# Joined shift copies, a shared Gelu session and a new planning string in a two-layer transformer kernel

## The chip, the cores and the metric

The kernel runs on one core of one Trainium2 chip. The metric is the device time of one execution in microseconds; less is better. The kernel before has a median of 1543.89 us over three runs.

## The reference

Two layers, each made of softmax attention and a two-matrix network, with a residual around each and a layer normalisation before each. Both layers use the same weights. The input x is 2048 tokens of 512 channels in bf16; there are 32 heads of 16 channels, and the hidden width F is 1376.

```python
def _A_ref(x, wqkv, wo):
    ...
    scores = jnp.einsum("bhqd,bhkd->bhqk", q, k) * scale
    p = _softmax(scores, axis=-1)
    o = jnp.einsum("bhqk,bhkd->bhqd", p, v)
    return o.transpose(0, 2, 1, 3).reshape(B, S, D) @ wo

def _B_ref(x, w1, b1, w2, b2):
    y = _layernorm(x, axis=-1)
    h = _gelu(jnp.einsum("bsd,df->bsf", y, w1) + b1)
    return jnp.einsum("bsf,fd->bsd", h, w2) + b2

x = A_x
x = x + _A_ref(_layernorm(x, axis=-1), A_wqkv, A_wo)
x = x + _B_ref(_layernorm(x, axis=-1), B_w1, B_b1, B_w2, B_b2)
# and the same two steps once more
```

## The kernel before

The program is not written out by hand. A planner in Python (the class `Sched`) runs while the kernel is built: jobs, written as generators, hand it tasks for TensorE (pe), ScalarE (act), VectorE (dve), GpSimd (pool) and SyncE (sp, the DMA queue), each with a priority (lower goes first), a planned duration and the buffers it reads and writes. `best` picks for every engine the task of best priority among those that are ready by the engine's planned free time plus a small look-ahead (0.05 us on VectorE). The result is one fixed instruction stream per engine with semaphore waits; at run time nothing is chosen any more. So a planned duration moves instructions in the order, and has no other effect. A second pass (`refill`) puts multiplications by zeros into planned holes of TensorE's stream.

**The score tiles.** The work is cut into segments: for each layer (called 1 and 3 in the code), each unit of query tokens (up to 512; layer 3's last unit is cut into 256, 128 and 128) and each group of four heads. A segment has a tile of 128 keys x 512 queries for every key block and head. There are 4096 such tiles of exponentials in all, and two ways to make one.

- ScalarE: an Exp over three or two score banks at once (line 1493), written to the buffer `PT`. One multiplication per tile then accumulates it with V (line 1701).
- VectorE, for five of every sixteen key blocks only: `d_load` (line 1594) turns the scores of one tile into bit patterns of bf16 numbers, by adding a constant and writing integers. A pair of tiles (`DBATCH` is 2) fills one slot u of the buffer `dp`, 1024 integers a partition. `job_d` then makes the shifted copies: a first shift (line 1625) writes slot u+1 as slot u plus a constant, 1024 elements; a second shift (line 1630) writes the two slots v, v+1 as slots u, u+1 plus another constant, 2048 elements. A tile so made is accumulated four times, with V and three scaled copies of V (`vs`). A few pairs are closed half filled, and their shifts have half the elements.

`flow_scores` decides at each step, tile by tile, which engine gets the next ones (`take_d`, `d_solo`), by the planned backlog of VectorE and the free slots. Its thresholds come from the class `Hint`: every fourth group of ScalarE reads one character of the string `ORDER`, which picks one of ten sets of thresholds (`MODES`). The string has 315 characters.

**Priorities on VectorE.** A score eviction has 0.0, the transpose that empties the accumulator bank 0.3, a shift 2.5 as a rule, and 0.5 or 0.15 when its segment runs out.

**The rest of a layer.** `job_segend` normalises a segment, `job_post` multiplies by wo, adds the residual, normalises again, and starts `job_ffn` for the unit. `job_ffn` multiplies by w1 chunk by chunk (`mm_w1`, line 1836), adds the bias on VectorE (line 1860) into the buffer `h16`, and then runs Gelu over the whole buffer on ScalarE (lines 1875 and 1876). Exp and Gelu need different tables, so each such session stands between two table loads. The multiplication by w2 follows (line 1883), then the residual (line 1885) and, for layer 3, the store of the output. There is one `h16`, so a unit's session must be over before the next unit's chunks come in. `job_tail` does the same for the last 128 tokens in its own way.

**Buffers.** `dp` has 14 slots of 1024 integers; the second half of the buffer `OT`, a tensor of its own, is lent as two more (14 and 15) in the middle of each layer. Free slots, in pairs, are handed out in the order in which they were freed. `qk` and `xnT` are buffers for making q, k and v, and are not used after layer 3's are made.

Of the kernel before, what the change touches and what calls it, by code (L numbers as in the profile page):

```python
# [63 lines left out]
class Prog:  # L64


    def __init__(self):
        self.streams = {e: [] for e in ENGINES}
        self.last_writer = {}
        self.readers = {}  # L70
        self.ops = []
        self.dma_rr = 0
        self.free = {e: 0.75 for e in ENGINES}
        self.bus = 0.0
        self.spare = tuple
        self.tiling = "full"
        self.tiles = {}
        self.drain = 0.0
        self.hit = (0.0, 0.0, 0.0)
        self.work = []  # L80
# [25 lines left out]
    def op(self, eng, fn, reads=(), writes=(), same_ok=(), dur=0.3, lat=None):  # L106
# [32 lines left out]
        else:  # L139
            if eng == "pool":  # L140
                self.hit = (op.t0, op.t0 + dur, lat or 0.0)
                lat = None
            elif lat == "fast":
                if self.hit[0] < op.t0 + dur and op.t0 < self.hit[1]:
                    dur += self.hit[2]
                lat = None
# [109 lines left out]
class Task:  # L256

    __slots__ = ("eng", "ops", "prio", "cb", "seq")

    def __init__(self, eng, prio, ops):  # L260
        self.eng = eng
        self.prio = prio
        self.ops = ops
        self.cb = None
        self.seq = 0

# [12 lines left out]
class Sched:  # L279
# [80 lines left out]
    def release(self, name, slot):  # L360
# [5 lines left out]
        if p.waiters:  # L366
            _, _, cb = heapq.heappop(p.waiters)
            cb(slot)
        else:
            p.free.append(slot)  # L370

# [74 lines left out]
    def run(self):  # L446
        while True:
# [19 lines left out]
            for (fn, reads, writes, same_ok, dur, lat) in t.ops:  # L467
                self.P.op(t.eng, fn, reads, writes, same_ok, dur, lat)
            if t.cb is not None:
                t.cb()  # L470
# [6 lines left out]
AHEAD = 0.3  # L477
HOLD_REACH = 1.0
# [40 lines left out]
DOT = True  # L519


class Hint:
    BASE = dict(D_IDLE=1.2, PV_LEAST=0.75, HOLD_LATE=0.4, PV_NEAR=0.7, LIN2=9, D_STEAL=0)
    MODES = (dict(), dict(D_IDLE=0.8), dict(D_IDLE=1.7), dict(PV_LEAST=0.6), dict(PV_LEAST=0.9), dict(HOLD_LATE=0.2), dict(HOLD_LATE=0.6), dict(PV_NEAR=0.4), dict(LIN2=0.9), dict(D_STEAL=1.0))
    STEP = 4
    ORDER = '503313558500015300210144501302104000000301040403092343050392450495084100003032530945249044022459044803755795410000404059000042073300979450905900455532342400007300030045005594475501306437245071003021030010012714080892409008554010031403031302434070022009444030045044310000030072220934002201909240590090394095010099504'
# [13 lines left out]
class Builder:  # L540
# [45 lines left out]
    def alloc(self, es):  # L586
# [31 lines left out]
        self.dp = t("dp", [128, NDP, 1024], U16)  # L618
        self.vs = t("vs", [128, 3, 3, len(DK), 68], BF16)
        self.OT = t("OT", [128, 8, 512], BF16)  # L620
# [85 lines left out]
    def otd(self, hg):  # L706

        return [("dp", NDP + (hg - 4) // 2, w) for w in (0, 1)] if DOT and hg >= 4 else []

    def dpu(self, u):  # L710

        return self.dp[:, u, :] if u < NDP else self.OT[:, 2 * (u - NDP) + 4:2 * (u - NDP) + 6, :].rearrange("p a n -> p (a n)").bitcast(U16)

    def dpp(self, u):

        return self.dp[:, u:u + 2, :] if u < NDP else self.OT[:, 4:8, :].rearrange("p a n -> p (a n)").bitcast(U16).rearrange("p (u n) -> p u n", u=2)
# [143 lines left out]
    def flow_weights(self):  # L860
# [17 lines left out]
        for qc in range(self.NC + 1):  # L878
            L = 1 if qc < self.NC else 3
            if qc:  # L880
                yield ("keys", [("post", 1, qc - 1)])
            for fc in range(self.NFC):
                yield first(fc)
                S_.mark(("w1", L, qc % self.NC, fc))
            if L == 1:
# [14 lines left out]
    def ln_group(self, tiles, slot, prio, eps1, eps0, shift):  # L900
# [14 lines left out]
        if shift:  # L915
            nmr = self.nmr[:, c0:c0 + n]
            yield Task("pool", prio, [I(lambda e: e.tensor_tensor(out=nmr, in0=self.mv[:, c0:c0 + n, 0], in1=rs, op=ALU.mult), [R] + [("mv", c0 + i) for i in range(n)], [("nmr", slot)], 0.2),
                                      I(lambda e: e.tensor_scalar(out=nmr, in0=nmr, scalar1=-1.0, scalar2=None, op0=ALU.mult), [("nmr", slot)], [("nmr", slot)], 0.2)])
# [142 lines left out]
    def bound(self, x, y, a, c, ns, dst, RQ, RN, prio, eng):  # L1061
# [4 lines left out]
        yield Task("dve", prio, [I(lambda e: e.tensor_scalar(out=yi, in0=x.bitcast(I32), scalar1=-0.5, scalar2=RSQRT_MAGIC, op0=ALU.mult, op1=ALU.add), RN, [RY], 0.18)])  # L1066
        yield Task(eng, prio, [I(lambda e: e.tensor_tensor(out=a, in0=x, in1=y, op=ALU.mult), RN + [RY], [RA], 0.25 if pool else 0.2)])
        yield Task(eng, prio, [I(lambda e: e.tensor_tensor(out=c, in0=a, in1=y, op=ALU.mult), [RA, RY], [RC], 0.25 if pool else 0.2)])
        yield Task(eng, prio, [I(lambda e: e.tensor_scalar(out=c, in0=c, scalar1=-0.5, scalar2=1.5, op0=ALU.mult, op1=ALU.add), [RC], [RC], 0.217 if pool else 0.2)])
        yield Task(eng, prio, [I(lambda e: e.tensor_tensor(out=a, in0=a, in1=c, op=ALU.mult), [RA, RC], [RA], 0.25 if pool else 0.2)])  # L1070
        yield Task(eng, prio, [I(lambda e: e.tensor_scalar(out=dst, in0=a.rearrange("p (n o) -> p n o", o=1), scalar1=-MARG, scalar2=0.0, op0=ALU.mult, op1=ALU.add),
                                    [RA], [RQ], 0.333 if pool else 0.2)])
# [108 lines left out]
    def job_scl(self, L, part, prio):  # L1181
# [19 lines left out]
        yield Task("dve", prio, [I(lambda e: e.tensor_scalar(out=self.krhs[:, :], in0=self.mask8[:, :], scalar1=self.kmx[:, 1:2], scalar2=None, op0=ALU.mult), [("kmx", 1), ("mask8",)], [("krhs",)], 0.1)])  # L1201
# [23 lines left out]
    def job_qt(self, sg, s):  # L1225
# [9 lines left out]
                                  [RS, ("scl", k), ("qbias",)], [("qt", q)], 0.16 + 0.24 * W / 512 if eng == "dve" else 0.41 + 0.48 * W / 512, (), "fast" if eng == "dve" else 0.09)])  # L1235
# [8 lines left out]
    def job_vs(self, sg, i, kbs):  # L1244
# [9 lines left out]
        if L == 1:  # L1254
# [5 lines left out]
                                   [("V", hg, kb) for kb in kbs], [("vs", q, i + k2) for k2 in range(n)], 0.209 + 0.17 * n, [("vs", q, i + k2) for k2 in range(n)] if k > 1 else [], 0.09) for k in (1, 2, 3)])  # L1260
# [321 lines left out]

    def close_batch(self):
# [35 lines left out]
    def job_d(self, bt):  # L1619
# [5 lines left out]
        yield Task("dve", prio(), [I(lambda e: e.tensor_scalar(out=self.dpu(u + 1)[:, 0:N], in0=self.dpu(u)[:, 0:N], scalar1=float(SHIFT[1]), scalar2=None, op0=ALU.add),  # L1625
                                     [("dp", u, w) for w in range(n)], [("dp", u + 1, w) for w in range(n)] + self.dres(u + 1), 0.150 + 0.2605e-3 * N, (), "fast")])
        self.d_ready(bt, 1, u + 1, u, range(n))
        v = yield ("get", "dp", sg["i"])
        self.need2 -= 1
        yield Task("dve", prio(), [I(lambda e: e.tensor_scalar(out=self.dpp(v)[:, :, 0:N], in0=self.dpp(u)[:, :, 0:N], scalar1=float(SHIFT[2]), scalar2=None, op0=ALU.add),  # L1630
                                     [("dp", u + i, w) for i in (0, 1) for w in range(n)], [("dp", v + i, w) for i in (0, 1) for w in range(n)] + self.dres(v) + self.dres(v + 1), 0.150 + 0.521e-3 * N, (), "fast")])
        for i in (0, 1):
# [91 lines left out]
    def job_segend(self, sg):  # L1724
# [15 lines left out]
        if nparts == 2 and part == 0:  # L1740
            yield Task("dve", 1.2, [I(lambda e: e.tensor_copy(out=self.rowA[:, hg, :], in_=T[:, :, 17]), [RA], [("rowA", hg)], 0.17)])
# [5 lines left out]
        if nparts == 2:  # L1747
# [4 lines left out]
            yield Task("pool", 1.2, [I(lambda e: e.tensor_tensor(out=M, in0=M, in1=dw.unsqueeze(2).broadcast_to([128, 16, 16]), op=ALU.mult), [RW] + RO, RO, 0.62, (), 0.28),  # L1752
# [30 lines left out]

    def post_prio(self, L, qc):

        return 0.95 if L == 1 and qc >= self.NC - 2 or L == 3 and qc >= LATE3 else 2.2

    def job_post(self, L, qc):
# [28 lines left out]
        if self.prev(L, qc):  # L1817
# [14 lines left out]
    def mm_w1(self, L, qc, fc, b, pr, W, y0=0):  # L1832
        M = 128 if fc < self.NFC - 1 else self.FLAST
        yield ("keys", [("w1", L, qc, fc)])
        for c0 in (0, 2):
            yield Task("pe", pr if c0 == 0 else min(pr, HINT.LIN2), [I(lambda e, c=c: e.matmul(self.ps[0:M, b, 0:W], lhsT=self.w1(fc, c), rhs=self.yT[:, c, y0:y0 + W], start=(c == 0), stop=(c == 3)),  # L1836
# [7 lines left out]
    def job_ffn(self, L, qc):  # L1844
# [6 lines left out]
        hv = self.gv  # L1851
        yield ("keys", [("retq", 2), ("retq", 3), ("rets", 1)])
        for fc in range(NFC):
# [6 lines left out]
            S_.submit(Task("dve", pr - 0.7, [I(lambda e, fc=fc, M=M, b=b: e.tensor_scalar(out=hv[0:M, fc * W:(fc + 1) * W], in0=self.ps[0:M, b, 0:W], scalar1=self.b1c[0:M, fc:fc + 1], scalar2=None, op0=ALU.add),  # L1860
                                               [("ps", b), ("b1c",)], self.hres(fc * W // 512), 0.2 + 0.54 * W / 512, [("h", fc * W // 1024)])]),
                      cb=lambda b=b, fc=fc: (S_.release("mb", b), S_.mark(("h", L, qc, fc))))
        S_.mark(("ffn1", L, qc))
        yield ("keys", [("h", L, qc, fc) for fc in range(NFC)])
        HR = [("h", k) for k in range((NFC * W + 1023) // 1024)]
# [9 lines left out]
        yield Task("act", -1.0, [I(lambda e: e.activation(out=self.gv[:, 0:nf * W], in_=hv[:, 0:nf * W], func=ACTF.Gelu_apprx_tanh), HR, HR, (0.2 if last else 1.5) + 0.427 * nf * W / 512, (), (0.2 if last else 1.513) + 0.427 * nf * W / 512),  # L1875
# [3 lines left out]
        for i, tt in enumerate(tiles):  # L1879
            yield ("ready", "pe", GR + [r for fc in range(NFC) for r in self.w2res(L, fc)])  # L1880
            b = yield ("get", "mb")
            for f0 in range(0, NFC, 2):
                yield Task("pe", pr if f0 == 0 else min(pr, HINT.LIN2), [I(lambda e, fc=fc, i=i, b=b: e.matmul(self.ps[:, b, :], lhsT=self.gt(fc, i, W), rhs=self.w2(L, fc), start=(fc == 0), stop=(fc == nf)),  # L1883
                                        GR + self.w2res(L, fc), [("ps", b)], 0.216, [("ps", b)]) for fc in range(f0, min(f0 + 2, NFC))])
# [197 lines left out]
```

## Time and profile before

| | |
|---|---|
| median of three runs (lowest, highest) | 1543.89 us (1541.95, 1544.90) |
| the profiled execution, own time | 1542.35 us |
| its span, first to last instruction | 1540.5 us |
| ScalarE: exponentials, L1493 | 1258 instructions, 1421.4 us |
| ScalarE: all Gelu over `h` and `g`, L1875 and L1876 | 18 instructions, 40.0 us |
| ScalarE: table loads | 18, of 1283 ns each |
| VectorE: score evictions, L1594 | 983 instructions, 655.7 us |
| VectorE: first shifts, L1625 | 495 instructions, 210.5 us |
| VectorE: second shifts, L1630 | 495 instructions, 342.7 us |

In the profile's groups a line number names the line of the kernel that issued the instruction; engines are PE (TensorE), PEld (its weight loads), DVE (VectorE), ACT (ScalarE), POOL (GpSimd), SP (the DMA queue). Durations are those of single instructions, and neighbours on one engine can overlap, so sums of durations can exceed the time taken. The buffer `h16` appears as `h`, `g10` as `g`. The profiler's spans of GpSimd are rough.

### The profile page before, as it was taken

How to read it: one execution, taken by the hardware profiler on the slowest of the kernel's cores; microseconds unless marked ns; L12 is line 12 of the kernel's file. 1: busy time of each engine (PE TensorE's matmuls, PEld its weight loads, DVE VectorE, ACT ScalarE, POOL GpSimd, SP SyncE). 2: the span in 40 equal slices, each digit the busy share in tenths (PEclk: the TensorE clock that was granted, in tenths of full speed). 3: DMA queues.
4: the chain of work that ended last, by engine and by line, in shares of the span. 5: the costliest groups of instructions: out<-in, count | busy, mean ns of one | idle time of the engine just before them, and what ended most of it. 6: DMA issues, size and time to landing. Idle time of an engine off the chain costs nothing.

```text
span 1540.5 us, 41172 instructions
## 1 busy us (share of the span) xinstructions
PE 1490.5 (97%) x17581; PEld 489.7 (32%) x17581; DVE 1459.9 (95%) x2857; ACT 1505.1 (98%) x1348; POOL 331.0 (21%) x570
## 2 busy tenths in 40 slices
PE   8999999999999999999999999999999999999998
PEld 3222222222222222232222322222222222344565
DVE  8899999999999899999999898999999999999896
ACT  8999999999999999999999999999999999999997
POOL 3686322001220021102322217320001000020200
PEclk9999999999999999999999999999999999999999
DMA  6673012213311132223832332310101100221221
GB/s 164 118 157 87 26 29 35 55 31 76 87 46 48 41 69 74 60 49 82 153 51 62 64 69 71 62 25 22 29 19 36 35 18 24 41 41 33 66 67 30
DMA packets 212488, 90.56 MB, mean 59 GB/s; under 512 B 182251, under 2 KB 207184, under 8 KB 212304
## 3 DMA queue, kind: packets, MB, share of 16 engines
q1 hardware_dynamic: 212304, 87.92, 26.0%
q8 instruction: 138, 2.26, 0.6%
q14 instruction: 46, 0.38, 0.1%
HBM read 36.81 MB, written 19.48 MB: 37 GB/s over the span
## 4 chain that ended last, share of the span: by engine, by line
ACT 47%; DVE 25%; PE 23%; issue 2%; POOL 2%; DMA 1%; SPq 0%; POOLq 0%; DVEq 0%
ACT PT L1493 44%; DVE dp L1594 9%; PE ps L1508 7%; PE ps L1701 6%; DVE dp L1630 4%; PE ps L1883 3%; DVE dp L1625 2%; PE ps L988 2%; ACT h L1875 2%; PE ps L1836 2%; PE ps L1397 1%; DVE accT L1731 1%; DVE n L1053 1%; DVE h L1860 1%; DVE OT L1594 1%
## 5 line engine op out<-in xcount | busy, mean ns | idle before, releaser
L1493 ACT ACTIVATE PT<-ps 128x1536 bf16<-128x1536 f32 (+1 forms) x1258 | 1421.4, 1302 | 19.8 <-PE ps L1508 16.8
L1594 DVE TENSOR_SCALAR dp<-ps 128x512 uint16<-128x512 f32 x899 | 599.2, 682 | 32.6 <-PE ps L1508 29.9
L1508 PE MATMUL ps<-QT,KT 32*128 32x512 bf16 (+2 forms) x5120 | 602.1, 339 | 24.5 <-ACT PT L1493 7.4
L1701 PE MATMUL ps<-PT,V 128*17 128x512 bf16 (+2 forms) x3891 | 478.0, 338 | 0.1
L1701 PE MATMUL ps<-dp,vs 128*17 128x512 bf16 (+2 forms) x3377 | 438.9, 336 | 1.5 <-issue 0.6
L1508 PEld LDWEIGHTS ps<-QT,KT 32*128 32x128 bf16 x5120 | 175.0, 91 | 543.1 <-ACT PT L1493 290.9
L1630 DVE TENSOR_SCALAR dp<-dp 128x2048 uint16<-128x2048 uint16 x404 | 280.5, 699 | 2.9 <-PE ps L1701 0.2
L1234 POOL TENSOR_SCALAR QT<-qraw,scl,qbias 128x512 bf16<-128x512 bf16 (+2 forms) x91 | 73.0, 802 | 813.8 <-PE ps L1508 811.1
L1701 PE MATMUL ps<-dp,V 128*17 128x512 bf16 (+2 forms) x1135 | 210.8, 337 | 1.3 <-DVE accT L1731 0.7
L1625 DVE TENSOR_SCALAR dp<-dp 128x1024 uint16<-128x1024 uint16 (+1 forms) x453 | 192.7, 436 | 2.3
L1701 PEld LDWEIGHTS ps<-dp,vs 128*17 128x17 bf16 x3377 | 115.7, 89 | 110.5 <-issue 81.0
L1701 PEld LDWEIGHTS ps<-PT,V 128*17 128x17 bf16 x3891 | 122.6, 89 | 87.8 <-issue 71.4
L1401 PE MATMUL ps<-zw 128*32 128x448 bf16 (+21 forms) x1389 | 150.1, 323 | 0.3 <-DVE dp L1594 0.2
L1399 PE MATMUL ps<-zw 32*128 32x444 bf16 (+5 forms) x379 | 117.6, 331 | 0.0
L1836 PE MATMUL ps<-yT,wf 128*128 128x512 bf16 (+5 forms) x440 | 101.5, 340 | 2.7 <-DMA yT<-xn 1.4
L1397 PE MATMUL ps<-zw 128*128 128x448 bf16 (+15 forms) x382 | 96.8, 341 | 3.1 <-DVE onec L783 2.1
L988 PE MATMUL ps<-wqkv,xnT 128*128 128x512 bf16 x336 | 93.7, 382 | 3.9 <-DVE qk L1001 1.0
L1701 PE MATMUL ps<-OT,vs 128*17 128x512 bf16 (+2 forms) x310 | 79.0, 360 | 0.0
L1860 DVE TENSOR_SCALAR h<-ps,b1c 128x512 bf16<-128x512 f32 (+4 forms) x99 | 65.6, 666 | 4.5 <-PE ps L1836 3.9
L1259 POOL TENSOR_SCALAR vs<-V 128x340 bf16<-128x340 bf16 (+2 forms) x72 | 62.4, 867 | 29.8 <-PE ps L1701 20.9
L1701 PEld LDWEIGHTS ps<-dp,V 128*17 128x17 bf16 x1135 | 52.7, 88 | 34.0 <-issue 17.5
L1731 DVE STREAM_TRANSPOSE accT<-ps 128x512 f32<-128x512 f32 (+2 forms) x96 | 59.3, 618 | 2.3 <-PE ps L1701 2.3
(197 smaller groups left out, 1169.4 us busy)
## 6 DMA issues: line engine op xcount, KB each, us to landing
vs<-vs_scr SPq DMA_DIRECT2D x64, 255.0 KB, 2.8
wf<-in_B_w_dram SPq DMA_DIRECT2D x90, 128.0 KB, 2.4
q_scr<-qk SPq DMA_DIRECT2D x20, 256.0 KB, 2.0
k_scr<-qk SPq DMA_DIRECT2D x12, 256.0 KB, 2.0
out_dram<-xres SPq DMA_DIRECT2D x16, 128.0 KB, 1.7
vs_scr<-vs SPq DMA_DIRECT2D x8, 255.0 KB, 2.7
xres<-in_A_x_dram SPq DMA_DIRECT2D x7, 256.0 KB, 3.6
v_scr<-vst SPq DMA_DIRECT2D x12, 136.0 KB, 1.9
```

Source lines behind the costliest of these rows:

```text
L988: yield Task("pe", prio if c0 == 0 else min(prio, HINT.LIN2), [I(lambda e, c=c: e.matmul(self.ps[:, b, :], lhsT=xnT[:, c, :], rhs=self.wqk ...
L1397: fn = lambda e: e.matmul(self.ps[:, b, 0:w], lhsT=self.zw[:, 0:128], rhs=self.zw[:, 0:w], start=st, stop=st, skip_group_check=True)
L1399: fn = lambda e: e.matmul(self.ps[:, b, 0:w], lhsT=self.zw[32 * p:32 * p + 32, 0:128], rhs=self.zw[32 * p:32 * p + 32, 0:w], start=st, sto ...
L1401: fn = lambda e: e.matmul(self.ps[32 * p:32 * p + 32, b, 0:w], lhsT=self.zw[:, 0:32], rhs=self.zw[:, 0:w], start=st, stop=st, skip_group_c ...
L1493: S_.submit(Task("act", 1e-5 * gi, [I(lambda e, pt=pt, n=n, b0=b0: e.activation(out=self.PT[:, pt:pt + n, :], in_=self.ps[:, b0:b0 + n, :] ...
L1508: return [I(lambda e, kb=kb, i=i: e.matmul(self.ps[:, b, i * W:(i + 1) * W], lhsT=self.KT[32 * hp:32 * hp + 32, hg, kb * 128:(kb + 1) * 12 ...
L1594: self.S_.submit(Task("dve", 0.0, [I(lambda e: e.tensor_scalar(out=self.dpu(u)[:, w * 512:(w + 1) * 512], in0=self.ps[:, b, :], scalar1=BI ...
L1625: yield Task("dve", prio(), [I(lambda e: e.tensor_scalar(out=self.dpu(u + 1)[:, 0:N], in0=self.dpu(u)[:, 0:N], scalar1=float(SHIFT[1]), sc ...
L1630: yield Task("dve", prio(), [I(lambda e: e.tensor_scalar(out=self.dpp(v)[:, :, 0:N], in0=self.dpp(u)[:, :, 0:N], scalar1=float(SHIFT[2]), ...
L1701: ops.append((nth[j, sh] + 0.1 * i, I(lambda e, hp=hp, v=v, ap=ap[:, i * W:(i + 1) * W], first=first and i == 0, W=W: e.matmul(self.ps[32 ...
L1836: yield Task("pe", pr if c0 == 0 else min(pr, HINT.LIN2), [I(lambda e, c=c: e.matmul(self.ps[0:M, b, 0:W], lhsT=self.w1(fc, c), rhs=self.y ...
L1860: S_.submit(Task("dve", pr - 0.7, [I(lambda e, fc=fc, M=M, b=b: e.tensor_scalar(out=hv[0:M, fc * W:(fc + 1) * W], in0=self.ps[0:M, b, 0:W] ...
```

## The change

1. **Joined shifts.** A shift task of a whole pair carries a mark (`mate`): its kind and its slots. When the planner issues one, it looks for another of the same kind on VectorE that is ready within the look-ahead and whose slots stand in the same order; if there is one, both go out as one instruction over two pieces of memory (`both`, `d_join`), planned 0.15 us shorter than the sum. For this `dp` and `OT` become one tensor `bits` (18 slots, the lent pair is now 16 and 17), and free pairs are handed out lowest first.
2. **Shared session.** `HELD` names layer 3's unit 0 as held for unit 1. Unit 0's biased chunks go into `qk` and `xnT`; its Gelu, w2 multiplication, residual and stores follow with those of unit 1, in one session between two table loads. Two short memsets prepare the row that carries the second bias. Unit 1 no longer waits for the end of unit 0.
3. **Planner.** The model of how GpSimd slows a VectorE instruction looks at GpSimd's last four instructions instead of one. Some twenty planned durations change by 0.02 to 0.3 us, nearly all upwards.
4. **String and priorities.** `Hint` gets two more modes (`POST`), which change the priority of `job_ffn`'s multiplications, and a new `ORDER` of 315 characters, 60 of them as before at their place. After the last score group w1 multiplications get priority 1.3, and the last-but-one unit's residual additions 3.0.

```diff
@@ Sched.release
             p.free.append(slot)
+            if name == "dp":
+                p.free.sort()
@@ Prog.op
             if eng == "pool":
-                self.hit = (op.t0, op.t0 + dur, lat or 0.0)
+                self.hits = self.hits[-3:] + [(op.t0, op.t0 + dur, lat or 0.0)]
...
-                if self.hit[0] < op.t0 + dur and op.t0 < self.hit[1]:
-                    dur += self.hit[2]
+                dur += sum(h for t0, t1, h in self.hits if t0 < op.t0 + dur and op.t0 < t1)
@@ Sched.run
+            both = None
+            if t.mate is not None:
+                lim = max(pick[0], self.P.free["dve"]) + self.LOOK["dve"]
+                both = next((o for o in self.pend["dve"] if o.mate is not None and o.mate[0] == t.mate[0] and (o.mate[1] < t.mate[1]) == (o.mate[2] < t.mate[2]) and self.task_ready(o) <= lim), None)
+            if both is not None:
+                self.pend["dve"].remove(both)
+                (fn, reads, writes, same_ok, dur, lat), more = t.ops[0], both.ops[0]
+                x, y = sorted((t.mate[1:], both.mate[1:]))
+                self.P.op("dve", self.join(t.mate[0], x, y), reads + more[1], writes + more[2], same_ok, dur + more[4] - SHIFT_FIXED, lat)
+                for o in sorted((t, both), key=lambda o: o.mate[1:]):
+                    o.cb()
+SHIFT_FIXED = 0.15
+HELD = {(3, 0): (3, 1)}
@@ Builder
+    def both(self, a, b, o=None):
+        if o is not None:
+            return self.bits[:, a + o:b + o + 1:b - a, :]
+        return self.bits[:, :, :].rearrange("p (u a) n -> p u (a n)", a=2)[:, a // 2:b // 2 + 1:(b - a) // 2, :]
+    def d_join(self, kind, x, y):
+        if kind == 1:
+            return lambda e: e.tensor_scalar(out=self.both(x[0], y[0], 1), in0=self.both(x[0], y[0], 0), scalar1=float(SHIFT[1]), scalar2=None, op0=ALU.add)
+        return lambda e: e.tensor_scalar(out=self.both(x[1], y[1]), in0=self.both(x[0], y[0]), scalar1=float(SHIFT[2]), scalar2=None, op0=ALU.add)
@@ job_d
+        if n == DBATCH:
+            t.mate = (1, u, u)
...
+        if n == DBATCH:
+            t.mate = (2, u, v)
@@ job_ffn
+        if held:
+            yield ("keys", [("lent", L, k) for k in range(5)])
+            yield Task("dve", 2.0, [I(lambda e: e.memset(self.hc(nf)[self.FLAST:128, :], 0.0), [], [("hx",), ("xnT", 2)], 0.3),
+                                    I(lambda e: e.memset(self.hc(nf)[self.FLAST:self.FLAST + 1, :], 1.0), [], [("hx",), ("xnT", 2)], 0.3)])
...
+        if held:
+            return
         yield ("keys", [("h", L, qc, fc) for fc in range(NFC)])
+        if pair:
+            yield ("keys", [("h",) + pair + (fc,) for fc in range(NFC)])
...
+        held_acts = [A(self.qk[:, s, :, :].rearrange("p a n -> p (a n)"), [("qk", s, 0), ("qk", s, 1)], 4) for s in (0, 1)] + [A(self.xnT[:, 0:2, :, :].rearrange("p s c t -> p (s c t)"), [("xnT", 0), ("xnT", 1)], 2), A(self.hc(nf), [("xnT", 2)], 1, self.FLAST)] if pair else []
...
-        for i, tt in enumerate(tiles):
+        for i, tt in [(i - 4, tt) for i, tt in enumerate(self.units[L][pair[1]] if pair else ())] + list(enumerate(tiles)):
@@ Hint and its users
-    BASE = dict(D_IDLE=1.2, PV_LEAST=0.75, HOLD_LATE=0.4, PV_NEAR=0.7, LIN2=9, D_STEAL=0)
+    BASE = dict(D_IDLE=1.2, PV_LEAST=0.75, HOLD_LATE=0.4, PV_NEAR=0.7, LIN2=9, D_STEAL=0, POST=0)
...
+    def soft(self, pr):
+        return 1.1 if HINT.POST == 1 and 0.95 <= pr < 2 else 0.95 if HINT.POST == 2 and pr > 2 else pr
@@ mm_w1
+        if y0 == 0 and ("scores_done",) in self.S_.done:
+            pr = 1.3
@@ planned durations, examples
-        yield Task("dve", prio, [I(lambda e: e.tensor_scalar(out=self.krhs[:, :], ...), [("kmx", 1), ("mask8",)], [("krhs",)], 0.1)])
+        yield Task("dve", prio, [I(lambda e: e.tensor_scalar(out=self.krhs[:, :], ...), [("kmx", 1), ("mask8",)], [("krhs",)], 0.22)])
```

## The prediction

> **What bounds the kernel now.** I read the page first (busy time, the chain that ended last, the costliest groups), then the waits, the busy time of 40 stretches, and the timelines of VectorE and ScalarE at single places.
>
> ```profile
> span 1540.5 us, 41172 instructions
> ...
> PE 1490.5 (97%) x17581; PEld 489.7 (32%) x17581; DVE 1459.9 (95%) x2857; ACT 1505.1 (98%) x1348; POOL 331.0 (21%) x570
> ...
> PEclk9999999999999999999999999999999999999999
> ...
> ACT 47%; DVE 25%; PE 23%; issue 2%; POOL 2%; DMA 1%; SPq 0%; POOLq 0%; DVEq 0%
> ```
>
> Three engines look full. PE's figure holds 2150 multiplications by zeros put into holes (L1397, L1399, L1401: 364.5 us), and the granted clock is full in every slice, so PE is not the limit. ScalarE and VectorE share one job, the 4096 score tiles: ScalarE takes 3113 (598 instructions on three tiles, 659 on two, one on a single tile), VectorE 983. ScalarE has the largest share of the chain and the least slack: 35.4 us of the span idle, VectorE 80.6. By the stretches 9.2 us of ScalarE's idle time lie before 154 us and 9.6 from 1501 us on, which leaves 16.6 between; VectorE's are 15.8, 15.3 and 49.5.
>
> **The exchange rate.** A gain on one engine counts only as tiles are shared out anew.
>
> ```profile
> 1075.34 169.78 ACT PT L1493 x151
> ```
>
> ```profile
> 1070.39 2.48 DVE L1594 TENSOR_SCALAR dp<-ps 128x512 uint16<-128x512 f32 x4
> ```
>
> The first line is the longest piece of the chain (start, length, count): 151 exponentials in 169.78 us, 1.124 us each, at 2.5 tiles 0.45 us a tile. The second, from VectorE's timeline, has four score evictions in 2.48 us, the first 0.68, so each further one 0.60; half of a first shift (0.33) and of a second (0.60), found below, make 1.07 us a tile. Moving x tiles from ScalarE to VectorE shortens the end by 0.45x and costs VectorE 1.07x plus the 0.45x of span it loses: 1 us freed on VectorE is worth 0.45/1.52 = 0.30 us at the end. One us freed on ScalarE is worth T with T + 0.45T/1.07 = 1: 0.70 us.
>
> **Part 1, joined shifts.** The kernel makes two shift instructions per pair of tiles: 1024 elements, then 2048 (488 whole pairs). The change makes one instruction of two that are ready together.
>
> ```profile
> 1072.79 0.75 DVE L1625 TENSOR_SCALAR dp<-dp 128x1024 uint16<-128x1024 uint16 x2
> 1073.45 0.68 DVE L1594 TENSOR_SCALAR dp<-ps 128x512 uint16<-128x512 f32 x1
> 1074.05 0.68 DVE L1630 TENSOR_SCALAR dp<-dp 128x2048 uint16<-128x2048 uint16 x1
> 1074.65 0.69 DVE L1630 TENSOR_SCALAR OT<-dp 128x2048 uint16<-128x2048 uint16 x1
> 1075.25 0.42 DVE L1625 TENSOR_SCALAR dp<-dp 128x1024 uint16<-128x1024 uint16 x1
> ```
>
> Durations and starts differ here, and it decides the price. Two first shifts of 0.42 end after 0.75 us: the second starts 0.33 after the first, so 0.08-0.09 of each lies under its neighbour. A second shift starts 0.60 after the other. A joined first shift has 2048 elements, so 0.60 in place of 2 x 0.33 = 0.66 to 0.67: it saves 0.07. A joined second shift, by 0.27 per further 1024 elements, takes 0.60 + 0.54 = 1.14 in place of 1.20: 0.06. By durations it would be 2 x 0.42 - 0.69 = 0.15, the upper bound. The lower: a second shift that reads what the instruction just ahead writes loses the overlap (about 0.1); two pairs in turn hide this behind each other, a joined pair of pairs does not, which eats the saving of two joins, so 0.
>
> The two pieces do not lie together in memory. The nearest row has that form, 2 pieces of 512 with a gap (second shift of half-filled pairs): 418 ns, against 424 for 1024 in one piece. I take no loss.
>
> [...]
>
> How many? In the order of VectorE's instructions, 64 times two whole first shifts and 45 times two second shifts stand side by side: 109 joins at least, if both were ready. Counting loads against shifts, 138 first shifts ran while a second loaded pair was waiting, 168 second shifts while another had its first: as a join uses two of the latter, 138 + 84 = 222 at most. A joined instruction starts when the later of the two may, 0.05 us at most behind; the accumulations that read the first pair's copies get them 0.27 to 0.54 later than now, and PE, which holds zeros to spare, hides that. A second join also needs both targets free and in the order of their sources. I take 160: 160 x 0.07 = 11 us of VectorE, x 0.30 = 3.3 us; bounds 0 and 222 x 0.15 x 0.30 = 10.
>
> **Part 2, the shared activation session.** Layer 3's unit 0 keeps its hidden tiles in idle buffers and goes through Gelu with unit 1.
>
> ```profile
> 1067.60 1.28 ACT L1875 ACT_TABLE_LOAD   x1
> 1068.89 4.47 ACT L1875 ACTIVATE h<-h 128x5120 bf16<-128x5120 bf16 x1
> 1073.40 0.63 ACT L1876 ACTIVATE g<-h 96x512 bf16<-96x512 bf16 x1
> 1074.05 1.28 ACT L1493 ACT_TABLE_LOAD   x1
> 1075.34 5.54 ACT L1493 ACTIVATE PT<-ps 128x1024 bf16<-128x1024 f32 x5
> ```
>
> This Gelu stretch goes away, and its elements join the one at 1246 us. Two table loads of 1.283 fall: 2.57 us. The elements now come in four pieces: 5120 take 4.472 and 2560 take 2.338, so 0.834 ns an element and 0.20 fixed; 2048, 2048, 1024 and 512 cost 1.91 + 1.91 + 1.06 + 0.63 = 5.51, against 5.10. ScalarE saves 2.16, x 0.70 = 1.5 us. [...] Two added memsets on VectorE (at most 0.45 each, the row of a 512-element bf16 operation) cost under 0.3. Unit 0's second multiplications (44 of 0.2 to 0.3 us) and four additions to the residual move from 1075 to about 1258 us, under the zeros PE does anyway; no score needs them. Uncovered, the 44 would cost some 10 us. No table or weight DMA is added; four output stores leave later, with some 280 us to spare.
>
> **Part 3, order and bookkeeping.** The new string, two new modes, softer priorities and new planned durations reorder all queues but change no other work. Putting the two buffers into one tensor costs nothing: same bytes, same addresses per instruction. What an order can recover is the idle time between start and tail: 16.6 us of ScalarE (x 0.70) and 49.5 of VectorE (x 0.30), at most 26 us together; it can lose as much. At the tail, the last-but-one unit's bias additions and residual additions step behind the tail's own chain: 0 to 1 us. The planned durations move towards the rows (a 0.1 becomes 0.22 where the row has 218 ns; a GpSimd 0.25 becomes 0.34 where it has 346), so fewer instructions should be planned to start before they can. I take a tenth: 2.5 us.
>
> **Sum.** 3.3 + 1.5 + 2.5 = 7.3 us off the profiled execution's 1542.35 (span 1540.5 and 1.85 around it): 1535.0. That execution is 1.5 under the median of the runs, 1543.89, so I state 1536.5. A measurement here tells apart about 0.2%, 3.1 us.
>
> **Rivals.**
>
> *Slower: the long instruction stands in the way.* A joined second shift holds VectorE 1.14 us where 0.60 was the most a shift did. Behind it queues the eviction of a score bank; PE, in order, waits for that bank, and ScalarE for the scores behind it.
>
> ```profile
> PEld ps L1508 <- DVE dp L1594: 67.8, 178, 1.3
> ...
> ACT PT L1493 <- PE ps L1508: 16.8, 38, 2.0
> ```
>
> The first row shows the wait exists, the second that little of it reaches ScalarE: 38 instructions of 1258. If each of about 60 joined second shifts passed its 0.54 on, that is 32 us of ScalarE, x 0.70 = 23. At one third it eats the 7.3; above 47% the kernel is slower by more than 0.2%; at two thirds it ends near 1552. For it speaks that nothing holds a join back when an eviction is about to come due; against it, that evictions have the first priority and two lanes.
>
> *No change.* Few joins come about (the ready-together test fails, or targets are out of order), VectorE's freed time stays idle as 49.5 us do now, and the order wins nothing: 1.5 us from part 2 and chance, 1541 to 1547, say 1543.
>
> *The order loses.* The doubled Gelu stretch stops exponentials for 7.74 + 5.51 = 13.2 us in one place; VectorE may run out of buffers for its tiles and both wait. 5.5 us, twice if the order is a poor one as well: 1547 to 1553.
>
> **Chances.** Forecast, faster by more than 0.2% (below 1540.8): 0.66. No change: 0.15. Long instruction: 0.12. Order loses: 0.07, making 0.19 for slower. The forecast's own range is 1526 to 1541 (joins at both bounds, the order 8 us either way). From 1524 to 1550 leaves out about half of the slower cases and a tenth of the faster.
>
> **What would show it.** Right: 110 to 220 joined shifts of 2048 and 4096 elements, starting 0.60 and 1.14 before the next; 14 table loads in the groups of L1493 and L1875's successors instead of 16; VectorE taking 10 or more tiles beyond 983; ScalarE's busy time down by about 7 us. Wrong: no such shapes; a joined shift well over 1.3 us; ScalarE's wait for scores above 17 us by ten or more; VectorE idle longer with the same 983 tiles.

## The result and the profile after

The change makes the kernel slower by 0.2%: a median of 1545.88 us over 20 runs (1543.17 to 1550.93) against 1542.51 us for the kernel before (20 runs, 1541.46 to 1544.90), a ratio of 1.0020, 95% interval 1.0013 to 1.0026. This is at the edge of what the measurement can tell; the forecast of 1536.5 and its sign were wrong. The profiled execution of after took 1543.17 us, the shortest of its runs; that of before (1542.35) lies at the middle of its own. So of the 3.4 us between the medians the two profiles hold only 0.9, the difference of their spans.

The page of after, its head, the chain's shares and the score evictions:

```profile
span 1541.4 us, 41484 instructions
...
PE 1490.7 (97%) x17809; PEld 491.4 (32%) x17809; DVE 1446.3 (94%) x2653; ACT 1503.9 (98%) x1346; POOL 346.7 (22%) x570
...
ACT 43%; PE 28%; DVE 23%; issue 2%; POOL 2%; DMA 1%; SPq 0%; POOLq 0%; DVEq 0%
...
L1628 DVE TENSOR_SCALAR dp<-ps 128x512 uint16<-128x512 f32 x982 | 651.6, 680 | 37.9 <-PE ps L1536 34.2
```

VectorE issues 204 instructions fewer and is busy 13.6 us less, as the change says. It makes 982 tiles, where it made 983. So its freed time bought no tile: 1541.4 - 1446.3 = 95.1 us of it stand idle, against 80.6 before. ScalarE is busy 1.2 us less and idle 2.1 us more (37.5 against 35.4), and that is the 0.9 us by which the span grew. PE's part of the chain rose from 23 to 28%.

The busy time between the start and the tail, first of before and then of after (columns: stretch, its length, busy time and instructions of PE, PEld, DVE, ACT and POOL, the granted clock, the DMA share, GB/s):

```profile
154.00:1501.00 1347.00, 1311.83 (x15640) 422.99 (x15638) 1297.51 (x2491) 1330.43 (x1173) 236.34 (x374) 1.00 0.24 51
```

```profile
154.00:1501.00 1347.00, 1311.26 (x15622) 422.18 (x15618) 1287.91 (x2292) 1326.57 (x1169) 252.85 (x382) 1.00 0.23 51
```

In the same 1347 us ScalarE works 3.9 us less and VectorE 9.6 us less. The middle has become looser on both engines that the prediction called full. Part of ScalarE's 3.9 has moved behind it: from 1501 us on it works 31.8 us, against 29.9 before.

The waits of after (who waited for whom: us in all, times, the longest):

```profile
PEld ps L1536 <- DVE dp L1628: 75.6, 202, 1.3
DVE dp L1628 <- PE ps L1536: 34.2, 55, 3.2
ACT PT L1521 <- PE ps L1536: 21.5, 43, 3.9
```

In before, tiles that land in the lent pair have rows of their own, under the name `OT`, which belong to the same waits:

```profile
DVE dp L1594 <- PE ps L1508: 29.9, 44, 3.3
...
PEld ps L1508 <- DVE OT L1594: 5.2, 14, 0.4
```

VectorE's wait for the scores of these 84 tiles is 1.5 us. Like for like, then, PE's wait for an eviction grew from 67.8 + 5.2 = 73.0 to 75.6 us, VectorE's wait for scores from 29.9 + 1.5 = 31.4 to 34.2, and ScalarE's from 16.8 to 21.5 with a longest single wait of 3.9 us where it was 2.0.

The joined shifts by form, and four lines of VectorE's timeline:

```profile
L1615 DVE TENSOR_SCALAR dp<-dp 128x4096 uint16<-128x4096 uint16 x98 | 122.6, 1253 | 0.1
L1614 DVE TENSOR_SCALAR dp<-dp 128x2048 uint16<-128x2048 uint16 x105 | 71.7, 684 | 0.0
```

```profile
889.03 0.68 DVE L1614 TENSOR_SCALAR dp<-dp 128x2048 uint16<-128x2048 uint16 x1
889.63 0.68 DVE L1628 TENSOR_SCALAR dp<-ps 128x512 uint16<-128x512 f32 x1
...
892.37 1.22 DVE L1615 TENSOR_SCALAR dp<-dp 128x4096 uint16<-128x4096 uint16 x1
893.50 0.68 DVE L1628 TENSOR_SCALAR dp<-ps 128x512 uint16<-128x512 f32 x1
```

There are 203 joins, with the next instruction 0.60 us behind a joined first shift and 1.13 behind a joined second one (medians over all of them: 0.599 and 1.133).

The shared session in ScalarE's timeline, and the table loads by form:

```profile
1257.97 1.28 ACT L1934 ACT_TABLE_LOAD   x1
1259.27 4.47 ACT L1934 ACTIVATE h<-h 128x5120 bf16<-128x5120 bf16 x1
1263.64 3.70 ACT L1932 ACTIVATE qk<-qk 128x2048 bf16<-128x2048 bf16 x2
1267.24 1.56 ACT L1932 ACTIVATE xnT<-xnT 128x1024 bf16<-128x1024 bf16 x2
1268.71 0.62 ACT L1935 ACTIVATE g<-h 96x512 bf16<-96x512 bf16 x1
1269.35 1.28 ACT L1521 ACT_TABLE_LOAD   x1
1270.64 4.63 ACT L1521 ACTIVATE PT<-ps 128x1536 bf16<-128x1536 f32 x4
```

```profile
L1934 ACT ACT_TABLE_LOAD x7 | 9.0, 1283 | 0.1
L1521 ACT ACT_TABLE_LOAD x7 | 9.0, 1283 | 0.1
```

Fourteen loads in these two groups, as the change says. The session takes 12.67 us between exponentials.

### The profile page after: what moved, and what is told of

Read it like the earlier page. It is cut to its first block, busy times and chain, and to the rows that moved or that the text cites. A ratio compares the mean times of both kernels' runs of the same rounds, so it can differ in the third digit from the quotient of the medians.

```text
span 1541.4 us, 41484 instructions
## 1 busy us (share of the span) xinstructions
PE 1490.7 (97%) x17809; PEld 491.4 (32%) x17809; DVE 1446.3 (94%) x2653; ACT 1503.9 (98%) x1346; POOL 346.7 (22%) x570
## 4 chain that ended last, share of the span: by engine, by line
ACT 43%; PE 28%; DVE 23%; issue 2%; POOL 2%; DMA 1%; SPq 0%; POOLq 0%; DVEq 0%
ACT PT L1521 40%; DVE dp L1628 10%; PE ps L1536 9%; PE ps L1741 9%; PE ps L1882 3%; PE ps L1943 3%; DVE dp L1667 2%; PE ps L1016 2%; DVE dp L1615 2%; ACT h L1934 1%; DVE dp L1659 1%; DVE dp L1614 1%; DVE accT L1771 1%; PE ps L1429 1%; DVE n L1081 1%
## 5 line engine op out<-in xcount | busy, mean ns | idle before, releaser
L1521 ACT ACTIVATE PT<-ps 128x1536 bf16<-128x1536 f32 (+1 forms) x1256 | 1423.3, 1286 | 24.9 <-PE ps L1536 21.5
L1628 DVE TENSOR_SCALAR dp<-ps 128x512 uint16<-128x512 f32 x982 | 651.6, 680 | 37.9 <-PE ps L1536 34.2
L1741 PE MATMUL ps<-dp,vs 128*17 128x512 bf16 (+2 forms) x3672 | 472.2, 339 | 0.9 <-DVE dp L1667 0.8
L1667 DVE TENSOR_SCALAR dp<-dp 128x2048 uint16<-128x2048 uint16 (+1 forms) x298 | 208.6, 701 | 3.2 <-PE ps L1741 0.7
L1429 PE MATMUL ps<-zw 128*32 128x448 bf16 (+17 forms) x1708 | 169.3, 326 | 1.1 <-DVE dp L1628 1.1
L1659 DVE TENSOR_SCALAR dp<-dp 128x1024 uint16<-128x1024 uint16 (+1 forms) x284 | 123.2, 435 | 2.5
L1615 DVE TENSOR_SCALAR dp<-dp 128x4096 uint16<-128x4096 uint16 x98 | 122.6, 1253 | 0.1
L1427 PE MATMUL ps<-zw 32*128 32x444 bf16 (+4 forms) x364 | 113.4, 331 | 0.0
L1425 PE MATMUL ps<-zw 128*128 128x448 bf16 (+20 forms) x321 | 80.7, 334 | 4.9 <-DVE dp L1628 2.3
L1614 DVE TENSOR_SCALAR dp<-dp 128x2048 uint16<-128x2048 uint16 x105 | 71.7, 684 | 0.0
L1741 PEld LDWEIGHTS ps<-dp,V 128*17 128x17 bf16 x1224 | 56.5, 88 | 40.7 <-issue 21.4
L1429 PEld LDWEIGHTS ps<-zw 128*32 128x32 bf16 x1708 | 59.4, 95 | 23.2 <-DVE dp L1628 3.7
```

The lines of the kernel that those rows point to most:

```text
L1427: fn = lambda e: e.matmul(self.ps[:, b, 0:w], lhsT=self.zw[32 * p:32 * p + 32, 0:128], rhs=self.zw[32 * p:32 * p + 32, 0:w], start=st, sto ...
L1429: fn = lambda e: e.matmul(self.ps[32 * p:32 * p + 32, b, 0:w], lhsT=self.zw[:, 0:32], rhs=self.zw[:, 0:w], start=st, stop=st, skip_group_c ...
L1521: S_.submit(Task("act", 1e-5 * gi, [I(lambda e, pt=pt, n=n, b0=b0: e.activation(out=self.PT[:, pt:pt + n, :], in_=self.ps[:, b0:b0 + n, :] ...
L1614: return lambda e: e.tensor_scalar(out=self.both(x[0], y[0], 1), in0=self.both(x[0], y[0], 0), scalar1=float(SHIFT[1]), scalar2=None, op0= ...
L1615: return lambda e: e.tensor_scalar(out=self.both(x[1], y[1]), in0=self.both(x[0], y[0]), scalar1=float(SHIFT[2]), scalar2=None, op0=ALU.add)
L1628: self.S_.submit(Task("dve", 0.0, [I(lambda e: e.tensor_scalar(out=self.dpu(u)[:, w * 512:(w + 1) * 512], in0=self.ps[:, b, :], scalar1=BI ...
```

## The experiments

**One planned duration.** Is the string bound to one exact plan? In before, one planned duration is changed, to the value that the change gives it; no instruction is added or taken away.

```diff
-        yield Task("dve", prio, [I(..., [("kmx", 1), ("mask8",)], [("krhs",)], 0.1)])
+        yield Task("dve", prio, [I(..., [("kmx", 1), ("mask8",)], [("krhs",)], 0.22)])
```

> The kernel before with one number changed: the planned duration of the small multiplication that makes krhs (four instructions in the whole program), 0.1 to 0.22 us, as in the change. No instruction is added, removed or resized by this edit; only the planner's order and the sharing of tiles follow. Theory A (the string fits one exact plan, and anything that shifts the plan by a little undoes its worth): slower by 30 to 60 us, 1575 to 1600, with some 15 tiles fewer on VectorE. Rival B (the string is worth what the prediction gave it, a few us): within 5 us of before.

Measured: 1583.15 us (1581.06 to 1583.89), ratio 1.0248 (1.0232 to 1.0263). The tiles on VectorE fall to 967. Its page and its largest wait of ScalarE:

```profile
span 1579.3 us, 41817 instructions
...
PE 1532.9 (97%) x17910; PEld 503.4 (32%) x17910; DVE 1455.0 (92%) x2831; ACT 1520.1 (96%) x1351; POOL 338.1 (21%) x570
```

```profile
ACT PT L1493 <- PE ps L1508: 39.1, 86, 3.7
```

A number that changes no instruction's work loses 38 us. Sixteen tiles go to ScalarE, which is busy 15.0 us more (7.2 of it by 0.45 us a tile) and idle 23.8 us more, nearly all of it waits for scores (39.1 us against 16.8). The string's worth is tied to the plan that it was found for: the time is that of the kernel with no string at all (below).

**No string at all.** The same two programs without the string's choices (before first, then after):

```diff
-    ORDER = '...'
+    ORDER = ''
```

> The kernel before with an empty string, so every step takes the first set of thresholds; nothing else is edited. Theory A (each string is worth tens of microseconds, and only in its own plan): about the time of the run with one changed duration, 1575 to 1600. Rival B (one changed duration did its harm by itself): nearer to before, under 1560.

> The changed kernel with an empty string; joins, shared session, priorities and durations stay. Theory A (the change's mechanics are worth their microseconds once both strings are taken away): 3 to 12 us faster than the kernel before with an empty string. Rival B (the mechanics do no good where nothing is tuned, and the new string had more to make up than the old): as slow as it or slower, 1590 to 1610.

Measured: before without a string 1584.76 us (1583.21 to 1586.40), ratio 1.0271 (1.0251 to 1.0291); after without one 1599.69 us (1599.39 to 1600.43), ratio 1.0368 (1.0348 to 1.0389). ScalarE's wait for scores in the first and in the second:

```profile
ACT PT L1493 <- PE ps L1508: 42.8, 82, 6.2
```

```profile
ACT PT L1521 <- PE ps L1536: 52.4, 95, 6.1
```

Both give VectorE 964 tiles; in the second, with 160 joins, it is busy 1447.2 us against 1451.0, and no tile comes of it. So the string is worth 2.71% in before (42 us) and 3.68 - 0.20 = 3.48% in after (54 us). Without strings the program of the change is 15 us behind, which was the rival's forecast.

**Strings found alike.** Is it the string or the program? Before, after, and after without its joins each get a string of their own, found by one and the same search (forward, twelve partial strings kept at each step, judged by the planner's own clock). For the last one, also:

```diff
-            t.mate = (1, u, u)
+            t.mate = None
...
-            t.mate = (2, u, v)
+            t.mate = None
```

> The kernel before with a string of my own, found by one forward search (12 partial strings kept at each step, 8 to 30 steps looked ahead, judged by the planner's own clock); nothing else is edited. A common yardstick for the next two, whose strings come from the same search with the same effort. All theories: much faster than the empty string (1584.8), slower than the delivered one (1542 to 1544): 1550 to 1565.

> The changed kernel with a string from the same search and effort as the run before it. Theory A (joins and shared session are worth 5 to 8 us once strings are equally good): 4 us or more faster than the kernel before under that search. Rival B (at equal search the mechanics are worth little, and the changed kernel's fate is its string's): within 4 us of it, on either side.

> The changed kernel without joins (no shift is marked for one; shared session, durations and priorities stay), again with a string from the same search. Theory A (joins give 3 us or more in a plan made for them): 3 us or more slower than the run before this one. Rival B (the planner finds as good an order without joins; undoing them cost time only because the order had been made for them): within 3 us of it.

| | median us | ratio to before (95%) | tiles on VectorE | VectorE busy | ScalarE's wait for scores |
|---|---|---|---|---|---|
| before | 1564.03 | 1.0118 (1.0102 to 1.0135) | 975 | 1459.7 | 31.4 |
| after | 1566.45 | 1.0129 (1.0110 to 1.0149) | 972 | 1442.5 | 36.6 |
| after, no joins | 1560.27 | 1.0091 (1.0073 to 1.0110) | 972 | 1457.6 | 30.1 |

With strings of like effort the programs lie within 0.4% of each other, after is not ahead, and the joins show no gain: the same 972 tiles with 15 us less work on VectorE, and a longer wait on ScalarE. That the kernel without joins comes out 6 us ahead of the one with them was in neither theory. The granted clock differs too: 0.992 to 0.995 in the runs of after, 0.995 to 0.999 without joins, 0.998 to 0.999 in before. Whether the lower clock makes the longer time or goes with it is not shown. And three programs are three draws of an order, so differences of 2 to 6 us between two of them are not put down to the change's parts.

**The joins undone in the order made for them.** After, with every joined instruction issued as its two halves, in the same place of the stream:

```diff
+                o.halves = (first.ops[0], second.ops[0])
@@ refill
+            if op.halves is not None:
+                for h in op.halves:
+                    x = P.op("dve", *h)
+            else:
                 x = P.op(*op.spec)
```

> The changed kernel with every joined shift issued as two instructions again, in the same place and order of all five streams (about 203 more VectorE instructions); string, priorities and shared session stay. Theory A (a join saves what the starts show, 0.07 us, on an engine that is full in places): 3 to 12 us slower than the changed kernel, so 1548 to 1558. Rival B (the long instructions stand in the way of evictions): 3 us or more faster than the changed kernel, below 1543. Rival C (VectorE's time is off the path): within 2 us of it.

Measured: 1554.63 us (1551.84 to 1559.99), ratio 1.0070 (1.0053 to 1.0087). The page and the wait:

```profile
PE 1505.9 (97%) x18004; PEld 498.8 (32%) x18004; DVE 1460.0 (94%) x2856; ACT 1506.6 (97%) x1346; POOL 342.8 (22%) x570
```

```profile
ACT PT L1528 <- PE ps L1543: 34.7, 65, 3.9
```

VectorE is busy 13.7 us more, the tiles stay at 982, ScalarE waits 13 us longer, and the time is 0.5%, about 8 us, above after's. The profiled execution is the slowest of the six, at a granted clock of 0.994 (after's had 0.998), so its waits are larger than those of the median run. The time is not down to the clock: the four runs at 0.998 have a mean of 1553.8 us, after's four at 0.998 one of 1544.9. The zeros are filled in anew, 195 more of them. So a join is worth something in an order that was planned around it.

**Joins alone, in before's order.** Before keeps its string and its streams; of VectorE's stream, 66 times two shifts that already stand side by side become one instruction.

```diff
@@ refill
+        joins, skip = self.find_joins(old)
...
-            x = P.op(*op.spec)
+            if id(op) in skip:
+                continue
+            x = P.op(*joins.get(id(op), op.spec))
```

> The kernel before with joins alone: string, durations and order stay, and where two whole shifts of one kind are neighbours in VectorE's stream and the second could already run at the first's place, they become one instruction (66 joins). Theory A (0.07 us each, 4.6 us of VectorE, but no tile changes engine since the sharing is fixed in the plan): within 2 us of before. Rival B (the first pair's copies come later and their readers wait): 3 us or more slower. Rival C (the prediction's exchange, 0.30 us a us, held without a new plan): 1.4 us faster.

Measured: 1542.30 us (1541.60 to 1543.76), ratio 0.9989 (0.9980 to 0.9997); 983 tiles, VectorE busy 1457.8 us, ScalarE's wait 18.0 us. That is 1.7 us less than before, with an interval of 0.5 to 3.1: theory A and rival C both fit it, rival B does not.

**Chosen joins.** The same, with 51 of the 66.

> Before's kernel and string, with 51 of the 66 neighbouring shift pairs made by one instruction in their old place; the 15 left apart are those behind whose second part something else was planned close. Theory A (a fixed order keeps what a join saves only where the instruction behind it on VectorE is next to limit the end): 51 x 0.07 = 3.6 us of VectorE's time fall, the tiles stay at 983, and of the time 1 to 3 us fall: 1539.5 to 1541.5 beside before's 1542.5, a little under the kernel that joined all 66 (1542.3 beside 1543.9). Theory B (what that kernel gained is the order's chance, not the joins): within 1 us of before.

Measured: 1541.27 us (1539.88 to 1543.98) beside 1545.07 for before, ratio 0.9978 (0.9970 to 0.9987). By their ratios this kernel is ahead of both before and after. Its page (the profiled execution lies at the top of its runs, and 134 records of PE are missing from it):

```profile
PE 1470.6 (95%) x17448; PEld 490.7 (32%) x17582; DVE 1456.7 (94%) x2806; ACT 1505.2 (98%) x1348; POOL 330.9 (21%) x570
```

VectorE is busy 3.2 us less than before's 1459.9 (51 x 0.07 = 3.6 was expected), and 0.22% of 1545 is 3.4 us at the end. Part of this goes with the granted clock: at 1.000 the eight runs of this kernel have a mean of 1540.5 us and before's four beside them 1542.8, which is 2.2 us. With 66 joins VectorE was busy 2.1 us less (4.6 was expected), and the end came 1.7 us sooner. The two intervals (2.0 to 4.6 us, and 0.5 to 3.1) overlap, so that choosing beats joining all is not shown.

**More zeros.** The profile of after has two stretches at half clock (below). Do they cost the time? After, with more multiplications by zeros in TensorE's holes:

```diff
-FILL_U = 0.55
+FILL_U = 0.75
```

> The changed kernel with the planned floor of TensorE's activity raised from 0.55 to 0.75, so about 580 more multiplications by zeros in holes; all other work keeps its order. Theory A (the stretches of half clock cost the changed kernel what its plan had won): granted clock 1.000 in the profile, and 3 to 7 us faster than the changed kernel, 1539 to 1543. Rival B (the half clock is a consequence of the waits, and costs little): clock as before the edit or higher, time within 2 us of the changed kernel.

Measured: 1546.47 us (1543.03 to 1549.99), ratio 1.0014 (1.0005 to 1.0024), a granted clock of 1.000 in the profile, and ScalarE's wait for scores is 21.4 us (47 times) where it was 21.5 (43 times). The time is as rival B forecast. ScalarE's timeline at two places, one behind the first stretch of half clock (684.3 to 687.7 us) and one at the second (1394.3 to 1397.7), of after and then with more zeros:

```profile
707.45 3.29 ACT L1521 ACTIVATE PT<-ps 128x1024 bf16<-128x1024 f32 x3 [2.24 <-PE ps L1536]
...
1397.12 4.63 ACT L1521 ACTIVATE PT<-ps 128x1536 bf16<-128x1536 f32 x4 [2.87 <-PE ps L1536]
```

```profile
707.35 3.28 ACT L1521 ACTIVATE PT<-ps 128x1024 bf16<-128x1024 f32 x3 [2.24 <-PE ps L1536]
...
1396.04 4.62 ACT L1521 ACTIVATE PT<-ps 128x1536 bf16<-128x1536 f32 x4 [0.90 <-PE ps L1536]
```

The stall 20 us behind the first stretch stands there at full clock too, and so does one of 1.2 us just ahead of it: they belong to the order. At the second stretch it is not so. PE goes on there at almost the same time (below), and the next exponential starts 2.45 us later in after and 1.40 at full clock, so about 1 us at this place goes with the half clock. The whole gained 0.2 us by the spans, and by the medians less than the intervals can tell. As the added zeros may have a price of their own, what the half clock costs after as a whole stays open.

## Why the prediction was wrong

**Part 3, the order, is the term that failed most.** It was entered as a gain of 2.5 us, "a tenth" of the idle time that an order can recover, with the sentence that it can lose as much. The runs show a term of another size: a string is worth 42 us in before and 54 in after, and before's string lost nearly all of that when one planned duration moved by 0.12 us (38 us). The change alters some twenty durations, the candidates of VectorE and the place of a session; its own string had to win back what before's had won, and it ended 3.4 us on the wrong side. With the joins undone in its own order after stands 0.70%, about 11 us, above before: without the joins, parts 2 and 3, entered as 1.5 + 2.5 = 4.0 us of gain, come to a loss of that size in this order. As that order was planned around the joins, the 11 us are no price for another one. The idle time bounds what a better order can gain on this kernel; the price of a worse one should have been bounded by the whole worth of the string, which no row of the profile of before shows.

**Part 1's price and count were right; its exchange rate is the second step that failed.** 203 joins (160 taken, 109 to 222 given), 0.60 and 1.13 us to the next start (0.60 and 1.14 expected), 13.6 us off VectorE (11 expected). The step "1 us freed on VectorE is worth 0.30 us at the end" needs tiles to move; 983 became 982; without strings it was 964 in both kernels, and with strings of like effort 972 with joins and 972 without. Who takes a tile follows from the plan and the string, and a plan with shorter shifts does not of itself hand VectorE more. Where no tile can move and the order stays (the chosen joins), 2.2 us of a saving of 3.2 reached the end at equal clock; where the order was made anew, the whole change lost. A join's worth lies in the waits of its order, in after about 8 us for 203, and not in tiles that move. Why a fixed order passes on more than 0.30 is open.

For neighbours on VectorE the starts give 2 x 0.60 - 1.13 = 0.07 us saved by a joined second shift, where 0.06 was expected.

**Part 2 held, at about its size.** Two loads of 1.283 us are gone, the pieces take 12.67 us from the first load to the next exponential where 13.2 was expected, and no gap between the session's rows is longer than 0.02 us. The two memsets take 0.49 and 0.27 us. ScalarE's busy time fell by 1.2 us; with one tile more on ScalarE (0.45) that is 1.65 like for like, against 2.16. Then its idle time rose by 2.1 and took it back. The session by itself was not measured.

**The rivals.** "No change" had the time (1541 to 1547) and half of the mechanism: VectorE's freed time stays idle and the order wins nothing, though not for want of joins. "The order loses" had the sign, but not the place: VectorE runs on through the doubled session (busy for 12.64 of its 12.67 us). "The long instruction stands in the way" was not it: the joins undone in place made the kernel slower. (Its threshold for a kernel slower by 0.2% comes out at 46%, not 47: 10.4 of 22.8 us.) Of the signs listed for "wrong", VectorE idle longer with the same tiles is what came; ScalarE's wait grew by 4.7 us, less than the ten named.

Of the 3.4 us themselves, the profiles hold 0.9 (2.1 us more idle time on ScalarE, with longer waits for scores, less 1.2 us of its work), and they do not show which of the change's edits put them there.

The rest goes along with a lower granted clock. After's runs have 0.996 to 0.999, with a mean of 0.9977. The 54 runs of before that stand beside the experiments have a mean of 0.9988, and in them 0.001 less goes with about 1.6 us more: means of 1542.6 us at 1.000, 1544.2 at 0.999, 1545.7 at 0.998 and 1547.4 at 0.997. After's runs have 1544.9, 1544.9 and 1547.1 at 0.999, 0.998 and 0.997, so at equal clock no clear difference is left. (For the 20 runs of before in the result no clock is known.) Whether after is slower because its clock is lower, or its clock is lower because PE waits more often, is not shown; with more zeros the mean clock rose to 0.9990, and the ratio fell only from 1.0020 to 1.0014.

## What to carry to other kernels

Where a planner's choices were searched for one exact program, an edit can throw away that whole search, as one planned duration did here: bound the edit by the search's whole worth (the same program with the choices removed tells it), before adding up what the instructions save. Time freed on an engine counts only if something can use it, so look for what decides the sharing of work, not only for what each unit of work costs. A small saving is best tried with the order held still: 51 joins in the old stream gained 0.22%, where the whole change, with 203 joins in a new order, lost 0.20%.

## What the hardware showed beside this

**Half clock in short stretches.** In the first 1541 us of after the granted clock is 0.5 twice, for 3.41 us each, where before had none. The busy time around the second (first line, the 3.4 us ahead of it; second line, the stretch):

```profile
1390.90:1394.30 3.40, 1.52 (x36) 0.58 (x28) 3.40 (x5) 3.35 (x4) 0.00 (x0) 1.00 0.33 76
1394.30:1397.70 3.40, 3.02 (x28) 0.98 (x28) 0.63 (x2) 0.57 (x1) 0.00 (x0) 0.50 0.00 0
```

PE had been busy for 1.52 of the 3.40 us ahead, and ahead of the first stretch for 2.86 of 3.40. What sets the half clock off is not shown.

**A late transpose.** What PE waited for there is, as the rows suggest, the last of four transposes of `yT`. Their time from issue to landing between 1386 and 1400 us:

```profile
DMA to landing us min/median/max: 2.4/2.5/4.8
```

The one that took 4.8 us was issued at 1389.50, so it landed at about 1394.3, and PE went on at 1394.67. The waits put this down to a VectorE shift in after (2.2 us), and with more zeros, where PE went on at 1394.64 (it was busy for 5.36 of the 6.00 us from 1394 on), to the transpose:

```profile
PE ps L1882 <- DMA yT<-xn: 1.3, 1, 1.3
```

The shift ended at 1394.40, later than the landing, but the multiplication reads nothing that it writes. ScalarE lost 2.87 us behind the wait in after, and 0.90 at full clock.

**Two pieces cost nothing here.** Of the 98 joined second shifts 13 read and write one piece of memory, 50 read and write two pieces with a gap, and 35 have the gap on one side; the median is 1.22 us for each kind.
